# A strip of scratch memory, a reordered key product and weight loads one step ahead, in a fused attention and channel-mix kernel

## The chip, the core and the metric

The kernel runs on one core of a Trainium2 chip. The metric is device time in microseconds (us): the median over runs of the whole program. Five engines work side by side: PE multiplies matrices, DVE, ACT and POOL work elementwise, SP issues most of the DMA transfers. Each runs its own instructions in the order in which they stand in the program, and waits for others by semaphores.

## The reference

```python
def _attn_ref(q, k, v, cap):                     # 8 batches, 12 heads, 448 positions, 64 wide
    scores = (1 / sqrt(64)) * q @ k.T
    scores = cap * tanh(scores / cap)
    attn = softmax(scores)                       # 1e-9 added to the sum
    return attn @ v
def _moe_ref(x, mu_k, mu_r, w_k, w_v, w_r):      # x: 8 x 448 x 768, the attention's output
    xk = mu_k * x + (1 - mu_k) * x_prev          # x_prev: the position before
    xr = mu_r * x + (1 - mu_r) * x_prev
    v = relu(xk @ w_k) ** 2 @ w_v                # 768 -> 1024 -> 768
    return sigmoid(xr @ w_r) * v
```

The weights come as 64-bit floats, and the kernel turns them into 32-bit ones itself.

## The kernel before

**Pairs and steps.** Two heads make a pair: six pairs to a batch, 48 in all. The main loop in `run` has 55 steps. A step `i` works on several pairs at once, and a string (`STEP_0` for steps 0 to 5, `STEP_6` for 6 to 14, `STEP` after that) lists by hand the order in which its operations are written on the engines:

- `S0` to `S3` (`scores`) are the scores of pair `i` on PE, `tanh` and `exp` the two passes over them on ACT, `red` the row sums on DVE, `V` (`values`) the product with v of pair `i - 1`;
- `gather`, `recip`, `rec_store` and `rec_load` carry the row sums of pair `i - 1` through DMA to DVE and back;
- `norm`, `mix_old`, `mix_new`, `x_high`, `x_low` make `xk` of pair `i - 2` and split it, on POOL, into a high part `xkh` and a low part `xkl`; `gate_old` (POOL) and `gate_new` (DVE) make `xg`, and `x_store` writes that, or for 14 pairs the raw `x`, to memory (tensor `raw_d`).

**The key product.** `K` stands four times in a step. Each call of `kpart` (L367) does 6 of a batch's 144 passes: for each of 8 column blocks `fc` and each of 6 pairs `dc` of the batch three matmuls, (wh, xh), (wl, xh) and (wh, xl). `key_order` lists the passes. A batch's first six passes are done by the last `K` of step 6b+6, passes 6 to 29 by the four of step 6b+7, passes 30 to 35 by the first of step 6b+8. The sixth pair of batch b is mixed and split in step 6b+7. When a column block is done, `relu` takes it out of its PSUM buffer on ACT (tile `ko`, L374); there are two such buffers (`kps`), so block 2 can begin when block 0 is out.

**Weights.** `w_k` comes in 11 pieces, at steps 0 to 10; `w_r` and `w_v` in 28, at steps 15 to 42. In its step a piece is loaded by SP near the step's start (`weight_load`, tile `w64`, three buffers; L398 or L403), and ACT takes its absolute value at the step's end (`weight_abs`, L410, into `wsq`), just ahead of the next step's first `tanh`. DVE's five operations on it (`f`, L429 to L437) and POOL's sum (L444) follow in the next step.

**The end of attention.** Behind the last pair the pools of attention are closed, and `w2_prep` makes 7 combinations of blocks of `w_v` in high and low parts (`wvh`, `wvl`), on ACT (L490) and DVE (L491), with two scratch tiles `w2s` of 3072 bytes a partition. They lie where the pools `up` and `xp` lay: `up` takes 5632 bytes, and behind it in `xp` lie `x0` and `x1`, which `x_store` still reads for pairs 46 and 47. A scratch tile waits for what used its bytes before. The last batch's key passes run meanwhile; then 112 units of products with `w_v` and `w_r` (`multiply`, L559) fill PE to the end.

Of the kernel before, what the change touches and what calls it, by code (L numbers as in the profile page):

```python
# [10 lines left out]
F32 = mybir.dt.float32  # L11
# [11 lines left out]
ND = DM // 128  # L23
# [6 lines left out]
P = 128  # L30
# [7 lines left out]
KEYS, REST = range(NWK), range(15, 15 + (ND + NF) * 2)  # L38
# [33 lines left out]
class Body:  # L72
# [263 lines left out]
    def key_order(self, last):  # L336

        t = lambda fc, d0, d1: [(fc, dc, p) for dc in range(d0, d1) for p in range(3)]
        e = ND - 1
        if last:  # L340
            new = t(0, 0, e - 1) + t(1, 0, e - 1) + t(0, e - 1, e) + t(1, e - 1, e) + t(2, 0, e) + t(3, 0, 3) \
                + t(0, e, ND) + t(1, e, ND) + t(3, 3, e) + t(2, e, ND) + t(3, e, ND)
            rest = range(4, NF)
        else:
            new = t(0, 0, e) + t(1, 0, e) + t(0, e, ND) + t(1, e, ND)
            rest = range(2, NF)
        return new + [x for fc in rest for x in t(fc, 0, ND)]

# [56 lines left out]
        self.w_next = n + 1  # L405

    def weight_abs(self):
        for n, w in self.w_raw:
            sq = self.wp.tile([P, WC], F32, name="wsq", bufs=3)[:, :w.shape[1]]
            self.nc.scalar.activation(sq, w[:, :, 1].bitcast(F32), AF.Abs)  # L410
            self.w_abs.append((n, w, sq))
        self.w_raw, self.w_goal = [], self.w_next

    def weight_rest(self):
        while self.w_used < self.w_goal:
# [236 lines left out]
    def step(self, i, KS):  # L652

        nk = 0
        if self.maxima and i < NPAIR:
            self.row_maxima(i)
        pair = dict(load_qk=i + 3, qk_high=i + 2, qk_low=i + 2, qk_rise=i + 2, load_v=i, S=i, tanh=i, exp=i, red=i)
        pair.update(dict.fromkeys("V gather recip rec_store rec_load".split(), i - 1))
        pair.update(dict.fromkeys("norm mix_old mix_new x_high x_low gate_old gate_new x_store".split(), i - 2))
        for op in (STEP_0 if i < 6 else STEP_6 if i < REST[0] else STEP).split():  # L660
            j = pair.get(op)
            op, g = (op[:-1], (int(op[-1]),)) if op[-1].isdigit() else (op, ())
            if op in pair:
                j = pair[op] if j is None else j
                if 0 <= j < NPAIR:
                    getattr(self, dict(S="scores", V="values").get(op, op))(j, *g)
            elif op == "K":
                n = ((i - LAG) * 4 + nk + 1) * KS
                if 0 <= n < B * NF * ND * 3:
                    self.kpart(n, n + KS)  # L670
                nk += 1
            elif op == "tail_open":
                self.tail_open(i)
            elif op == "f":
                if i <= NPAIR:
                    self.fill()
            elif op == "weight_load":
                if i in KEYS or i in REST:
                    self.weight_load()
            else:  # L680
                getattr(self, op)()

    def run(self):
# [7 lines left out]
        with ExitStack() as outer:  # L691
            def pool(name, bufs, stack=outer, **kw):
                return stack.enter_context(tc.tile_pool(name=name, bufs=bufs, **kw))
# [16 lines left out]
            xkp1 = pool("xkp1", 1, kst)  # L710
            self.up = pool("up", 2, ust)
            xp = pool("xp", 1, ust)
            self.xkp = [pool("xkp0", 1, est), xkp1]
            self.wp = pool("wp", 1, wst)
            self.rawp = pool("rawp", 2, ast, **right)
# [13 lines left out]
            self.qk_high(1)  # L729
            self.qk_low(1)  # L730
            self.load_qk(2)
            self.wgen = self.weight_round()
            self.W2, self.b12, self.src, self.ss, self.ops, self.ps, self.ev, self.got, self.vl = ({} for _ in range(9))
            tail = NPAIR + 1
# [123 lines left out]
```

## Time and profile before

| what | value |
|---|---|
| median of 3 runs | 931.31 us (930.99 to 934.17) |
| profiled execution, its own time | 934.75 us |
| its span, first to last instruction | 932.9 us |
| PE busy | 895.6 us, 96% |
| DVE busy | 734.8 us, 79% |
| ACT busy | 640.9 us, 69% |
| POOL busy | 384.2 us, 41% |

The span is what the rows of a trace add up to; 1.85 us of the profiled execution lie outside it. The profiled execution took 3.4 us more than the median. Starts and durations below are in us from the span's start. Busy PE is not PE at its peak, since the ends of matmuls are modelled and overlap.

### The profile page before, as it was taken

How to read it: one execution, taken by the hardware profiler on the slowest of the kernel's cores; microseconds unless marked ns; L12 is line 12 of the kernel's file. 1: busy time of each engine (PE TensorE's matmuls, PEld its weight loads, DVE VectorE, ACT ScalarE, POOL GpSimd, SP SyncE). 2: the span in 40 equal slices, each digit the busy share in tenths (PEclk: the TensorE clock that was granted, in tenths of full speed). 3: DMA queues.
4: the chain of work that ended last, by engine and by line, in shares of the span. 5: the costliest groups of instructions: out<-in, count | busy, mean ns of one | idle time of the engine just before them, and what ended most of it. 6: DMA issues, size and time to landing. Idle time of an engine off the chain costs nothing.

```text
span 932.9 us, 15106 instructions
## 1 busy us (share of the span) xinstructions
PE 895.6 (96%) x4986; PEld 718.0 (77%) x4986; DVE 734.8 (79%) x1254; ACT 640.9 (69%) x947; POOL 384.2 (41%) x329
## 2 busy tenths in 40 slices
PE   6888999999999999999999989999999999999996
PEld 3335766666676666666666778999999999999996
DVE  7999886878888888888877468788887766877775
ACT  6898888787787788878787456565655535555553
POOL 4564463666676676666664200000000013344430
PEclk9899999999999999999999989999999999999999
DMA  4556554566655666656653372754445636666663
GB/s 143 167 173 189 188 174 150 186 186 205 203 196 192 204 212 204 211 179 201 196 180 119 114 277 96 254 182 145 158 157 162 195 110 202 216 212 220 221 216 111
DMA packets 122567, 170.37 MB, mean 183 GB/s; under 512 B 22512, under 2 KB 106608, under 8 KB 122480
## 3 DMA queue, kind: packets, MB, share of 16 engines
q1 hardware_dynamic: 113264, 154.64, 52.5%
q10 hardware_dynamic: 9216, 14.68, 4.2%
q8 instruction: 41, 0.67, 0.3%
q14 instruction: 46, 0.38, 0.1%
HBM read 109.91 MB, written 56.60 MB: 178 GB/s over the span
## 4 chain that ended last, share of the span: by engine, by line
PE 42%; POOL 19%; DVE 11%; DMA 9%; issue 9%; SPq 5%; ACT 3%; ACTq 0%; DVEq 0%; POOLq 0%
PE ps L559 37%; POOL xg L311 5%; POOL qkl L96 5%; DMA sq<-r 4%; POOL xkl L96 4%; SPq L258 4%; PE kps L367 2%; DVE r L253 2%; POOL qkh L86 2%; POOL xkh L86 2%; POOL wsq L444 2%; DMA w<-wk 2%; DVE sr L262 2%; PE s L209 1%; DVE xg L305 1%
## 5 line engine op out<-in xcount | busy, mean ns | idle before, releaser
L253 DVE TRANSPOSE_TENSOR_REDUCE r<-p 128x28 f32<-128x896 f32 (+1 forms) x240 | 215.3, 911 | 11.6 <-ACT p L227 8.6
L227 ACT ACTIVATE p<-p,cap_t 128x896 f32<-128x896 f32 x192 | 182.2, 949 | 6.6 <-ACT pv L288 1.5
L217 ACT ACTIVATE p<-s,scl_t 128x896 f32<-128x896 f32 x192 | 173.1, 901 | 18.3 <-PE s L209 14.1
L367 PE MATMUL kps<-xkh,wkh 128*128 128x448 f32 x372 | 142.9, 384 | 8.8 <-ACT ko L374 8.2
L367 PE MATMUL kps<-xkh,wkl 128*128 128x448 f32 x372 | 137.4, 369 | 0.1
L367 PE MATMUL kps<-xkl,wkh 128*128 128x448 f32 x372 | 137.3, 369 | 0.0
L559 PE MATMUL ps<-wvh,hi 128*128 128x384 f32 x392 | 131.2, 335 | 1.8 <-ACT hi L543 1.2
L559 PE MATMUL ps<-wvl,hi 128*128 128x384 f32 x392 | 131.0, 334 | 0.0
L236 PE MATMUL pv<-p,rv 128*64 128x448 f32 x576 | 125.3, 572 | 1.4 <-DVE xk L293 1.4
L543 ACT CAST hi<-s 128x512 fp32r<-128x512 f32 (+1 forms) x112 | 63.6, 568 | 90.9 <-PE ps L559 76.6
L523 POOL TENSOR_TENSOR s<-src 128x384 f32<-128x384 f32 x14 | 14.3, 1021 | 268.7 <-DVE lo L544 257.2
L544 DVE TENSOR_TENSOR lo<-s,hi 128x512 fp32r<-128x512 f32 (+1 forms) x112 | 70.5, 629 | 57.6 <-ACT hi L543 41.8
L96 POOL TENSOR_TENSOR qkl<-rqk,qkh 128x960 fp32r<-128x960 f32 x47 | 106.3, 2261 | 17.0 <-ACT qkh L90 8.8
L209 PE MATMUL s<-qkh 64*128 64x448 f32 (+1 forms) x336 | 84.3, 441 | 17.5 <-ACT p L217 11.3
L444 POOL TENSOR_TENSOR wsq<-wa,wsq 128x384 f32<-128x384 f32 (+1 forms) x39 | 43.8, 1124 | 135.2 <-DVE wsq L437 135.2
L559 PE MATMUL ps<-wrh,hi 128*128 128x384 f32 x294 | 98.6, 335 | 0.3 <-DVE o L582 0.3
L559 PE MATMUL ps<-wrl,hi 128*128 128x384 f32 x294 | 98.5, 335 | 0.0
L209 PEld LDWEIGHTS s<-qkh 64*128 64x128 f32 (+1 forms) x336 | 37.0, 188 | 75.1 <-ACT p L217 28.9
L367 PEld LDWEIGHTS kps<-xkh,wkh 128*128 128x128 f32 x372 | 70.8, 190 | 30.1 <-issue 13.1
L543 ACT CAST hi<-src 128x512 fp32r<-128x512 f32 (+1 forms) x84 | 47.6, 567 | 62.3 <-PE ps L559 59.6
L236 PEld LDWEIGHTS pv<-p,rv 128*64 128x64 f32 x576 | 38.9, 142 | 65.2 <-issue 59.8
L559 PE MATMUL ps<-wvh,lo 128*128 128x384 f32 x392 | 83.7, 334 | 0.0
(96 smaller groups left out, 1786.7 us busy)
## 6 DMA issues: line engine op xcount, KB each, us to landing
rqk<-qk SPq DMA_DIRECT2D x47, 480.0 KB
k_d<-ko ACTq DMA_DIRECT2D x64, 224.0 KB
src<-k_d SPq DMA_DIRECT2D x56, 256.0 KB
rv<-v SPq DMA_DIRECT2D x48, 256.0 KB
r<-rec_d SPq DMA_DIRECT2D x96, 112.0 KB
v_d<-o SPq DMA_DIRECT2D x56, 192.0 KB
src<-x_d SPq DMA_DIRECT2D x42, 256.0 KB
vl<-v_d SPq DMA_DIRECT2D x56, 192.0 KB
```

Source lines behind the costliest of these rows:

```text
L96: {"p": self.nc.gpsimd, "v": self.nc.vector}[e].tensor_sub(*a)
L209: nc.tensor.matmul(s[:, h, 0:S], qk[a][p, k], qk[b][p, 0:S], start=(n == 0), stop=(n == 2))
L217: self.nc.scalar.activation(p32, self.S.pop((i, g))[:, :n, 0:S], AF.Tanh, scale=self.scl_t)
L227: self.nc.scalar.activation(p32, p32, AF.Exp, scale=1.0 if self.maxima else self.cap_t)
L236: nc.tensor.matmul(pv[p, 0:S], v[:, g, h, :], ph[:, h, :], start=(g == 0), stop=False)
L253: self.nc.vector.tensor_reduce(out=out, in_=p32[p, h].rearrange("p h (b k) -> p (h b) k", k=32), axis=mybir.AxisListType.X, op=ALU.add, ap ...
L311: self.nc.gpsimd.tensor_scalar(self.xg, self.X[i % 2][:, 0:S], self.om["r"][:, i % NP:i % NP + 1], None, op0=ALU.mult)
L367: nc.tensor.matmul(self.kps[fc][:, 0:S], w, m[:, dc, :], start=first, stop=last)
L444: {"p": self.nc.gpsimd, "v": self.nc.vector}[e].tensor_add(sq, f(a), sq)
L543: self.nc.scalar.copy(hi, x)
L544: self.nc.vector.tensor_sub(lo, x, f(hi))
L559: self.nc.tensor.matmul(o, a[:, c, :], w[:, c, :], start=first and k == 0, stop=last and k == len(todo) - 1, skip_group_check=True)
```

## The change

```diff
         else:
-            new = t(0, 0, e) + t(1, 0, e) + t(0, e, ND) + t(1, e, ND)
+            new = t(0, 0, e) + t(1, 0, e - 1) + t(0, e, ND) + t(1, e - 1, ND)
             rest = range(2, NF)
...
     def weight_abs(self):
-        for n, w in self.w_raw:
+        for n, w in [self.w_raw.pop(0)]:
...
             self.w_abs.append((n, w, sq))
-        self.w_raw, self.w_goal = [], self.w_next
+            self.w_goal = n + 1
...
             elif op == "weight_load":
+                if i + 1 in KEYS or i + 1 in REST:
+                    self.weight_load()
+            elif op == "weight_abs":
                 if i in KEYS or i in REST:
-                    self.weight_load()
+                    self.weight_abs()
...
             xp = pool("xp", 1, ust)
+            xp.tile([P, P], F32, name="apart")
...
             self.load_qk(2)
+            self.weight_load()
```

Three things change. A tile `apart` of 512 bytes a partition, which nothing uses, goes in front of `x0`. In batches 0 to 6 the second column block's passes for the fifth pair move behind the first block's passes for the sixth pair, so that pass 27 is the first that reads the sixth pair, where it was pass 30. And each weight piece is loaded one step earlier than its `weight_abs`, the first ahead of the loop.

On PE, in step 7 (6b+7 for batch 0), the last nine of the 24 passes before the two scores of step 8. The tile `kps` is a column block's buffer; before, all are of block 1 (`kps_896`):

```order
L367 MATMUL kps_896<-xkh_420,wkh_123 128x448
L367 MATMUL kps_896<-xkh_420,wkl_124 128x448
L367 MATMUL kps_896<-xkl_421,wkh_123 128x448
L367 MATMUL kps_896<-xkh_420,wkh_123 128x448
L367 MATMUL kps_896<-xkh_420,wkl_124 128x448
L367 MATMUL kps_896<-xkl_421,wkh_123 128x448
L209 MATMUL s_939<-qkh_773 128x448 x2
```

and now the last three are of block 0 (`kps_799`):

```order
L367 MATMUL kps_899<-xkh_423,wkh_123 128x448
L367 MATMUL kps_899<-xkl_424,wkh_123 128x448
L367 MATMUL kps_799<-xkh_423,wkh_123 128x448
L367 MATMUL kps_799<-xkh_423,wkl_124 128x448
L367 MATMUL kps_799<-xkl_424,wkh_123 128x448
L209 MATMUL s_945<-qkh_776 128x448 x2
```

Those last three are passes 27 to 29, block 0 with the sixth pair: they finish block 0 here, and stand in front of all that PE does in the next step.

On ACT, from the end of step 7 to the third tanh of step 8 (`p` are the probabilities, `wsq` the absolute value of a weight piece, `ko` a column block taken out of PSUM), before:

```order
L227 ACTIVATE p32_1_917<-p32_1_917,cap_t_172 128x448
L410 ACTIVATE wsq_922<-w64_822 128x768
L217 ACTIVATE p32_2_978<-s_939,scl_t_174 128x896
L227 ACTIVATE p32_2_978<-p32_2_978,cap_t_172 128x896
L217 ACTIVATE p32_2_984<-s_946,scl_t_174 128x896
L227 ACTIVATE p32_2_984<-p32_2_984,cap_t_172 128x896
L90 CAST qkh_987<-rqk_924 128x960
L217 ACTIVATE p32_2_995<-s_964,scl_t_174 128x896
L374 ACTIVATE ko_997<-kps_796 128x448
L374 ACTIVATE ko_999<-kps_896 128x448
```

and now:

```order
L227 ACTIVATE p32_1_920<-p32_1_920,cap_t_173 128x448
L374 ACTIVATE ko_925<-kps_799 128x448
L380 DMA k_d_63<-ko_925 128x448
L410 ACTIVATE wsq_928<-w64_725 128x768
L217 ACTIVATE p32_2_984<-s_945,scl_t_175 128x896
L227 ACTIVATE p32_2_984<-p32_2_984,cap_t_173 128x896
L217 ACTIVATE p32_2_990<-s_952,scl_t_175 128x896
L227 ACTIVATE p32_2_990<-p32_2_990,cap_t_173 128x896
L90 CAST qkh_993<-rqk_930 128x960
L217 ACTIVATE p32_2_1001<-s_970,scl_t_175 128x896
L374 ACTIVATE ko_1003<-kps_899 128x448
```

Block 0's `ko` has moved from behind the third tanh of step 8 to the end of step 7, in front of the weight piece's absolute value and of the first tanh of step 8.

On SP, in front of and within step 0 (`rqk` is q and k of a pair, `rv` its v, `w64` a weight piece, `sq` the gathered row sums), before:

```order
L159 DMA rqk_213<-qk 128x960
L163 DMA rv_215<-v 128x512
L398 DMA w64_217<-wk 128x3x256
L159 DMA rqk_267<-qk 128x960
L258 DMA sq_0_197<-r1_0_193 32x112 x4
```

and now:

```order
L159 DMA rqk_214<-qk 128x960
L398 DMA w64_216<-wk 128x3x256
L163 DMA rv_218<-v 128x512
L398 DMA w64_220<-wk 128x3x256
L159 DMA rqk_270<-qk 128x960
L258 DMA sq_0_198<-r1_0_194 32x112 x4
```

One piece more is loaded at the start, and from then on the load at the same place in a step is that of the next piece.

## Rows read from the trace of the kernel before

**Rows 1.** The page: shares of the span on the ending chain, by engine and line.

```profile
PE ps L559 37%; POOL xg L311 5%; POOL qkl L96 5%; DMA sq<-r 4%; POOL xkl L96 4%; SPq L258 4%; PE kps L367 2%; DVE r L253 2%; POOL qkh L86 2%; POOL xkh L86 2%; POOL wsq L444 2%; DMA w<-wk 2%; DVE sr L262 2%; PE s L209 1%; DVE xg L305 1%
```

**Rows 2.** Waits of PE: us in total, times, longest.

```profile
PE kps L367 <- ACT ko L374: 8.2, 3, 4.4
```

**Rows 3.** Timeline of PE, end of attention: start, us, [idle before <-releaser].

```profile
543.82 0.37 PE L367 MATMUL s<-xkl,wkh 128*128 128x448 f32 x1
548.62 0.74 PE L367 MATMUL kps<-xkh,wkh 128*128 128x448 f32 x1 [4.44 <-ACT ko L374]
...
565.89 0.37 PE L367 MATMUL kps<-xkl,wkh 128*128 128x448 f32 x1
567.47 0.45 PE L559 MATMUL ps<-wvh,hi 128*128 128x384 f32 x1 [1.21 <-ACT hi L543]
```

**Rows 4.** Timelines of SP, DVE and ACT, end of attention.

```profile
533.22 4.16 SPq L479 DMA_DIRECT2D wvl<-w_d  x8
537.43 1.05 SPq L324 DMA_DIRECT2D raw_d<-x  x2
...
545.57 0.96 DVE L491 TENSOR_TENSOR w2s<-wvl,w2s 128x768 f32<-128x768 f32 x1 [4.05 <-DMA raw_d<-x]
...
548.03 0.97 ACT L374 ACTIVATE ko<-kps 128x448 f32<-128x448 f32 x2
...
555.35 0.55 ACT L374 ACTIVATE ko<-kps 128x448 f32<-128x448 f32 x1 [0.97 <-PE kps L367]
...
557.16 0.96 DVE L491 TENSOR_TENSOR wvl<-wvl,wvh 128x768 fp32r<-128x768 f32 x1 [2.39 <-ACT wvh L490]
```

**Rows 5.** Stretches: us, busy PE, PEld, DVE, ACT, POOL (instructions), PEclk, DMA, GB/s.

```profile
536.00:543.00 7.00, 7.00 (x36) 6.36 (x35) 2.72 (x4) 2.31 (x3) 1.71 (x2) 1.00 1.03 364
549.00:554.00 5.00, 5.00 (x14) 4.43 (x14) 4.88 (x7) 4.04 (x8) 0.00 (x0) 0.50 0.84 287
```

**Rows 6.** Timelines: pass 29 on PE, sixth pair's `xkl` on POOL, steps 7, 13, 43.

```profile
80.61 0.36 PE L367 MATMUL kps<-xkl,wkh 128*128 128x448 f32 x1
...
84.56 1.16 POOL L96 TENSOR_TENSOR xkl<-xk,xkh 128x448 fp32r<-128x448 f32 x1
...
151.21 0.37 PE L367 MATMUL kps<-xkl,wkh 128*128 128x448 f32 x1
...
151.83 1.16 POOL L96 TENSOR_TENSOR xkl<-xk,xkh 128x448 fp32r<-128x448 f32 x1
...
478.35 0.36 PE L367 MATMUL kps<-xkl,wkh 128*128 128x448 f32 x1
...
480.24 1.15 POOL L96 TENSOR_TENSOR xkl<-xk,xkh 128x448 fp32r<-128x448 f32 x1
```

**Rows 7.** Waits of DVE, whole run, and the last of them on its timeline.

```profile
DVE xg L305 <- POOL xg L311: 26.9, 29, 1.1
...
524.51 0.68 DVE L305 SCALAR_TENSOR_TENSOR xg<-x,mu_r,xg 128x448 f32<-128x448 f32 x1 [0.95 <-POOL xg L311]
```

**Rows 8.** Waits of ACT, whole run, for the pieces of the key weights.

```profile
ACT wsq L410 <- DMA w<-wk: 5.9, 3, 2.4
```

**Rows 9.** Stretch from step 4 to step 11, columns as in group 5.

```profile
41.00:128.00 87.00, 76.35 (x410) 46.65 (x407) 79.91 (x128) 72.67 (x89) 48.35 (x41) 0.94 0.61 191
```

**Rows 10.** Timelines of PE and ACT, steps 3 and 4.

```profile
42.83 1.01 PE L236 MATMUL pv<-p,rv 128*64 128x448 f32 x2 [1.37 <-DVE xk L293]
...
48.68 1.01 ACT L217 ACTIVATE p<-s,scl_t 128x896 f32<-128x896 f32 x1 [0.58 <-PE s L209]
```

**Rows 11.** Timeline of ACT, ends of steps 7 and 10, and the chain's load.

```profile
83.90 0.95 ACT L410 ACTIVATE wsq<-w 128x768 f32<-128x768 f32 x1 [1.79 <-DMA w<-wk]
84.75 0.98 ACT L217 ACTIVATE p<-s,scl_t 128x896 f32<-128x896 f32 x1
...
120.99 0.96 ACT L410 ACTIVATE wsq<-w 128x768 f32<-128x768 f32 x1 [1.71 <-POOL qkl L96]
...
115.99 4.91 DMA w<-wk
```

## What the change will do to the time

> **What bounds the kernel now.** I read first the shares of the chain that ended last [rows 1]. Outside the products at the end (PE, L559, 37%) it runs through POOL's `xg`, `qkl`, `xkl`, `xkh` and `qkh`, the DMA of the row sums and SP's issue of it, and DVE's `r` and `sr`; PE's K passes and scores hold 2% and 1%. PE is nearly always busy, but in attention it is held to the pace of POOL, DVE and the row sums' DMA; at the end it is the bound itself. The list of waits has PE waiting for `ko` 8.2 us in three places, the longest 4.4 [rows 2]. The reader is to see where each sits and who is late there. A K pass that comes late in attention costs only what the other engines don't have in hand; a stop at the end costs in full.
>
> All sums are against the profiled execution's 934.75 us and are then laid on the median, 931.31, 3.4 lower.
>
> **The strip.** DVE's operation on the second scratch tile starts at 545.57, after 4.05 us idle for the DMA `raw_d<-x` [rows 4]. That store is issued by SP at 537.43, behind eight loads of `wvl` from 533.22 on, in the same queue. `w2s` takes 6144 bytes, `up` 5632: the second scratch lies 512 bytes deep in `x0`. With the strip of 512 bytes in front it ends where `x0` begins, and the wait for the store goes; left is that for the third of the eight loads. What follows from the 4.05 us now: ACT's high part waits for `w2s`, its two `ko` start at 548.03 behind it, PE has stopped after 544.19 and goes on at 548.62 with 4.44 us idle [rows 3, 4]. I take the DVE wait, **−4.1**, and what lies behind it: at 555.35 ACT waits 0.97 us for PE [rows 4], which a PE that comes earlier takes away, **−1.0**; together **−5.1**. Lower bound of the gain 4.1. Upper: PE's whole 4.44 and the clock behind it. In 549 to 554 the granted clock is 0.50, 1.2 GHz; 14 passes take 5.00 us, 0.36 each, where 536 to 543 at 1.00 shows 36 in 7.00, 0.19 each [rows 5]. Some 15 passes at 0.165 more are 2.5 us; so 4.44 + 2.5 = 7.0. I stay near the lower end because DVE and ACT share the work with the passes there (2.39 us of DVE waiting for ACT's `wvh` at 557.16 stay [rows 4]).
>
> The Trainium skill has a rule on this (Perfetto Trace Analysis, Matmul Optimizations): the matmul engine scales its power with use, so matmuls should run back to back. The 0.50 after the 4.44 us stop agrees with it. By that rule alone the term would be −7.0, by the row of DVE's wait −5.1.
>
> **27 passes.** Now PE's last three passes of step 6b+7 wait for the sixth pair's high and low part, with the next step's scores, values and K passes queued behind them. Against the trace: pass 29 starts at 80.61 in step 7, `xkl` of the sixth pair ends at 84.56 + 1.16 = 85.72, 5.1 us later. In step 13 it is 151.21 against 152.99, 1.78; in step 43, 478.35 against 481.39, 3.04 [rows 6]. The four batches between give 2.45, 2.11, 1.32 and 1.72 by the same rows. PE would stand still for these, 12.4 us in the six after the first.
>
> How much of it reaches the end? The steps from 15 to 47 run in a ring without PE: POOL's `xg`, DVE's `xg`, row sums out and back through DMA, DVE's reciprocal and `xk`, POOL's `xkh`, `xkl`. The chain says so [rows 1], and so does DVE's `xg`: it waits for POOL's 29 times, 26.9 us in all, 0.9 a step, and still 0.95 in one of the last [rows 7]. That is what DVE has in hand; PE, which feeds the row sums DVE works on, may fall behind by as much without the ring noticing. A stall only sets PE to the ring's time, and the next one is then measured from there; so they don't add up. The last counts: 3.04 less 0.95, **+2.1**. Bounds: 0, if the ring goes on untouched, and +12.4, if each is kept.
>
> Step 7 is not in that ring: there the start-up's pace still holds. ACT too is now queued there: `ko` of block 0 waits for pass 29, and behind it stand the piece's absolute value and the first tanh of step 8. 85.72 + 0.37 (pass) + 0.55 (`ko`, as at 555.35 [rows 4]) + 0.95 (`wsq` [rows 11]) and 0.4 for issuing its store, an estimate, is 88.0 against 84.75 for that tanh [rows 11]: **+3.2**, in round numbers 3. Doing `ko` here also spares ACT and PE their later waits for block 0 (PE's for `ko` in rows 2 are the two besides 4.44, 8.2 − 4.4 = 3.8); they lie inside the stall, and I count nothing for them.
>
> **Weights a step ahead.** The same pieces at the same place in SP's queue, one earlier in name; one more load, ahead of the loop. The buffers (three `w64`) suffice, as a piece is read one step after its load. SP's other transfers keep their order, except that one piece goes ahead of `rv` at the start and none is left for steps 10 and 42. That piece is 128 × 768 words, 393 KB, and at the 364 GB/s of [rows 5] takes 1.1 us; values are wanted a step later than scores, so I put it at nothing, with a bound of +1.1. What goes is ACT's waits for `w<-wk`: 5.9 us in three [rows 8], 2.4, 1.8 and 1.8, and 1.71 more in step 10, which the row puts down to POOL but where the chain shows the load, 115.99 + 4.91 = 120.90, against 120.99 [rows 11]. Which are worth something? The first lies in step 3: V of that step starts at 42.83 after DVE's `xk`, and a tanh of step 4 waits for PE at 48.68 [rows 10]; hidden. Those at steps 6 and 7 lie in front of the stall above, which ends later than they did; hidden. The last counts, −1.7. Thus the early part is 3.0 − 1.7 = **+1.3**. Bounds: between 41 and 128 DVE is busy 79.91 of 87.00 [rows 9], so at most −7.1 by freeing ACT; above, the stall at its full 5.1 with nothing back.
>
> The Trainium skill says to issue a DMA early and wait late, so that its fixed cost lies behind compute (DMA: Bandwidth & Descriptors, Rules for kernel authors). If all four waits came off the end, that would be 5.9 + 1.7 = 7.6; DVE's 7.1 caps it.
>
> **Sum:** −5.1 + 1.3 + 2.1 = **−1.7**: 933.05 for this execution, and 931.3 − 1.7 = **929.6** for the median.
>
> **Rivals.**
> *B, the stalls vanish.* With the loads early, POOL's and DVE's chain up to `xkl` also moves forward in steps 3 to 10, the stall at step 7 shrinks with it, and the middle stalls stay within what the ring has in hand. Then −7.1 and −5.1 remain: 931.3 − 12.2 = 919; with the stall half there, 922. For it: four waits on one engine's way [rows 8, 11]. Against: DVE's share [rows 9], tanh already waiting for PE in step 4 [rows 10].
> *C, slower: each stall is kept.* PE's standstill delays scores and with them DVE's row sums, by more than the 0.95 us that DVE's `xg` has in hand [rows 7]; then POOL, released by the same `xg`, is as late in each batch. +12.4 + 1.3 − 5.1 = +8.6: 939.9. It decides from a stall of 0.95 on; all six are over it [rows 6]. Against: a step's row sums are gathered only in the next step, so a late score has time. A fallen clock behind each stall, as in 549 to 554 [rows 5], would add to it.
> *D, the strip does nothing.* DVE waits in place of the store for the third `wvl` load, issued at about 534.5; if its landing is as late as the store's, the 5.1 stay: 931.3 + 1.3 + 2.1 = 934.7. Against: the eight loads are issued over 4.16 us, and the store comes behind all of them [rows 4]: five loads stand between the third and the store.
>
> **How the numbers follow.** A, the forecast, 0.52: 929.6, its own range 926 to 933.5 (the strip at 7.0 and the last stall at 0 make −1.9 − 2.1 more, 925.6; the middle at +6 makes 933.5). B 0.28, 919 to 922. C 0.12, around 939.9. D 0.08, 934.7. A difference of 0.5% (4.7 us) is about what a measurement can tell from none; the borders are 926.65 and 935.97. Faster: B, and 0.06 of A with both good ends, 0.34. Slower: C and a little of D, 0.13. Same: the rest, 0.53. The range from 920 to 937 leaves out the better third of B and most of C, 0.2.
>
> **What would show it.** Right: no wait of DVE L491 for `raw_d`, PE's stop before block 2 in the last batch gone or under 1 us, granted clock 1.00 there; PE's K passes wait for POOL `xkl` seven times, the first about 5 us, the sum of the rest less than 12; DVE's `xg` wait for POOL falls in number; ACT's waits for `w<-wk` gone. Wrong: the first slots' start (567.47 before [rows 3]) moves by more than 5 us, either way; a new wait of DVE for a load at the end; POOL waiting for DVE in the step after each stall (C); step 11's start 5 us or more earlier (B).

## The result and the profile after

The changed kernel takes **940.08 us** (median of 7 runs, 935.70 to 943.18), the kernel before 932.79 in the same count of runs: a ratio of **1.0076** (95% interval 1.0050 to 1.0102), 7.1 us slower. The forecast was 929.6 us, with a range of 920 to 937, counted from a median of three runs of the kernel before, 931.31 us; that of seven is 1.5 us higher. The profiled execution took 943.18 us, its span is 941.3 us; it is 3.1 us above its median, and we shall see where these come from. One of the ten runs of e10 (below), 1697.4 us, was in a slow state and is left out of its ratio.

The waits of PE, whole run (us in total, times, longest). There were none for `xkh` and `xkl` before, and the 8.2 us for `ko` [rows 2] have become 2.6:

```profile
PE kps L367 <- POOL xkh L86: 8.8, 4, 5.2
PE kps L367 <- POOL xkl L96: 3.0, 6, 0.6
PE kps L367 <- ACT ko L374: 2.6, 2, 1.5
```

The first two rows are the new stops in front of pass 27 and of pass 29, 11.8 us together. The timelines of PE and ACT show them (start, us, [idle before <-releaser]), in step 7, two of those behind it, and at the end:

```profile
87.70 0.74 PE L367 MATMUL kps<-xkh,wkh 128*128 128x448 f32 x1 [5.17 <-POOL xkh L86]
...
223.07 0.47 PE L367 MATMUL kps<-xkh,wkh 128*128 128x448 f32 x1 [1.52 <-POOL xkh L86]
...
224.32 0.47 PE L367 MATMUL kps<-xkl,wkh 128*128 128x448 f32 x1 [0.56 <-POOL xkl L96]
...
487.32 0.47 PE L367 MATMUL kps<-xkh,wkh 128*128 128x448 f32 x1 [1.83 <-POOL xkh L86]
...
488.56 0.55 PE L367 MATMUL kps<-xkl,wkh 128*128 128x448 f32 x1 [0.56 <-POOL xkl L96]
...
575.54 0.44 PE L559 MATMUL ps<-wvh,hi 128*128 128x384 f32 x1 [2.17 <-ACT hi L543]
...
89.71 0.54 ACT L374 ACTIVATE ko<-kps 128x448 f32<-128x448 f32 x1 [5.13 <-PE kps L367]
...
90.75 0.91 ACT L410 ACTIVATE wsq<-w 128x768 f32<-128x768 f32 x1 [0.50 <-ACT ko L374]
91.56 0.99 ACT L217 ACTIVATE p<-s,scl_t 128x896 f32<-128x896 f32 x1
```

And the stretches around the first stop, columns as in group 5 of the rows of before: the granted clock (the figure behind the five engines) is 0.50, 1.2 GHz, behind it. Between 93 and 545 us it falls only once more, to 0.50 from 489 to 492, behind the last of these stops.

```profile
80.00:87.00 7.00, 2.52 (x13) 2.00 (x11) 6.86 (x11) 4.46 (x6) 4.72 (x3) 0.93 0.65 205
87.00:92.00 5.00, 4.19 (x15) 2.60 (x15) 2.97 (x5) 1.80 (x3) 1.79 (x3) 0.50 0.70 214
```

The lists of DVE's and POOL's waits tell who else is late. `r`, the row sum of a pair's probabilities, waits for ACT more than twice as often as before, and POOL's `xkh` waits for `xk` 30 times for 21; the forecast named POOL's wait as a sign of rival C. `xg` hands back only 3.4 of its 26.9 us [rows 7] and waits as often as before. The rows of the changed kernel:

```profile
DVE xg L305 <- POOL xg L311: 23.5, 29, 1.1
DVE r L253 <- ACT p L227: 19.5, 31, 1.4
POOL xkh L86 <- DVE xk L293: 55.1, 30, 7.0
```

And of the kernel before:

```profile
DVE r L253 <- ACT p L227: 8.6, 13, 1.1
POOL xkh L86 <- DVE xk L293: 48.2, 21, 6.8
```

At the end DVE's 4.05 us for `raw_d` and PE's 4.44 us stop [rows 3, 4] are gone, and new waits stand there, on ACT's and DVE's timelines:

```profile
554.27 0.97 ACT L374 ACTIVATE ko<-kps 128x448 f32<-128x448 f32 x2
557.05 1.08 ACTq L380 DMA_DIRECT2D k_d<-ko  x2
558.18 1.57 ACT L490 CAST wvh<-w2s 128x768 fp32r<-128x768 f32 x2 [2.94 <-DMA src<-k_d]
...
559.77 1.83 DVE L491 TENSOR_TENSOR wvl<-w2s,wvh 128x768 fp32r<-128x768 f32 x2 [2.42 <-ACT wvh L490]
```

To see where the time went, the same events are laid side by side: the end of `xkl` on POOL, pair by pair, the first product of the end on PE, and the span. Pairs are counted from 1 in this table, so that pairs 12, 42 and 48 are a batch's sixth. The last kernel is the changed one with the old order of passes (e4, below).

| event | before | after | e4 | after − before | after − e4 |
|---|---|---|---|---|---|
| `xkl` of pair 5 | 72.30 | 75.48 | 73.24 | +3.2 | +2.2 |
| pair 8 | 109.50 | 116.68 | 109.36 | +7.2 | +7.3 |
| pair 12 | 152.98 | 156.86 | 151.57 | +3.9 | +5.3 |
| pair 42 | 481.39 | 488.50 | 479.25 | +7.1 | +9.3 |
| pair 44 | 503.25 | 513.13 | 501.13 | +9.9 | +12.0 |
| pair 48 | 539.47 | 549.84 | 537.56 | +10.4 | +12.3 |
| first product of the end | 567.47 | 575.54 | 564.06 | +8.1 | +11.5 |
| span | 932.9 | 941.3 | 929.2 | +8.4 | +12.1 |

So, by the last column, the time goes in step 7, slowly through the middle and in the last batch but one; the end gives 2.3 us back (567.47 − 539.47 = 28.0 before, 25.7 now). The 3.2 us at pair 5, ahead of every moved pass, are an execution's own: the changed kernel and e5 (below) have the same instructions up to step 12, and there pair 5's `xkl` ends 2.8 us earlier, at 72.67. Their rows for 60 to 68 us, first of the changed kernel, then of e5, differ in the granted clock:

```profile
60.00:68.00 8.00, 5.74 (x22) 1.92 (x26) 7.77 (x15) 6.05 (x9) 4.74 (x4) 0.63 0.68 206
```

```profile
60.00:68.00 8.00, 7.33 (x37) 3.38 (x38) 6.76 (x14) 7.07 (x9) 4.90 (x5) 0.79 0.70 216
```

That is about the profiled execution's distance to its median, 3.1 us, and it is left out of what follows.

### The profile page after: what moved, and what is told of

Read it like the earlier page. It is cut to its first block, busy times and chain, and to the rows that moved or that the text cites. A ratio compares the mean times of both kernels' runs of the same rounds, so it can differ in the third digit from the quotient of the medians.

```text
span 941.3 us, 15079 instructions
## 1 busy us (share of the span) xinstructions
PE 897.6 (95%) x4986; PEld 717.1 (76%) x4986; DVE 738.5 (78%) x1254; ACT 643.0 (68%) x947; POOL 384.0 (41%) x329
## 4 chain that ended last, share of the span: by engine, by line
PE 49%; DVE 14%; POOL 13%; DMA 7%; issue 6%; SPq 5%; ACT 4%; DVEq 0%; ACTq 0%; POOLq 0%
PE ps L559 37%; DMA sq<-r 4%; SPq L258 4%; PE kps L367 4%; PE pv L236 4%; POOL xg L311 4%; POOL xkl L96 4%; PE s L209 4%; DVE r L253 3%; POOL qkl L96 2%; DVE sr L262 2%; POOL xkh L86 2%; DVE xk L293 2%; DVE xg L305 2%; ACT p L217 1%
## 5 line engine op out<-in xcount | busy, mean ns | idle before, releaser
L217 ACT ACTIVATE p<-s,scl_t 128x896 f32<-128x896 f32 x192 | 173.0, 901 | 23.6 <-PE s L209 20.6
L367 PE MATMUL kps<-xkh,wkh 128*128 128x448 f32 x372 | 141.2, 380 | 11.5 <-POOL xkh L86 8.8
```

The costliest lines, as they stand in the source:

```text
L217: self.nc.scalar.activation(p32, self.S.pop((i, g))[:, :n, 0:S], AF.Tanh, scale=self.scl_t)
L367: nc.tensor.matmul(self.kps[fc][:, 0:S], w, m[:, dc, :], start=first, stop=last)
```

## The experiments

Three theories of the loss stood against one another. P: the moved passes alone make it. W: the weights a step ahead make a part of it. And within P: L, the forecast's, that only the last stall counts, against K, that each stall is kept. Each comparison is with the kernel before, run in turn on the same chip (934.2 to 934.9 us there), e1 to e8 on one chip and e9 to e12 on another. Four kernels take the change apart.

**e1_strip**: the tile `apart` alone.

```diff
             xp = pool("xp", 1, ust)
+            xp.tile([P, P], F32, name="apart")
```

> The strip alone, the rest as before. Theory P (the passes' order makes the loss) and theory W (the weights a step ahead make a good part of it) agree here: in the changed kernel the way from the last xkl to the first product of the end took 25.7 us for 28.0 before, so -2 us against before, 930.5 or so, and no DVE wait for raw_d. The forecast had -5.1. If the strip only gains behind the other changes, 0.

Measured: 0.9987 (0.9966 to 1.0007), −1.2 us, which can't be told from none.

**e2_p27**: the passes alone.

```diff
-            new = t(0, 0, e) + t(1, 0, e) + t(0, e, ND) + t(1, e, ND)
+            new = t(0, 0, e) + t(1, 0, e - 1) + t(0, e, ND) + t(1, e - 1, ND)
```

> The 27 passes alone. Theory P: all of the loss ahead of the end is this edit's, +5 by step 8, +2 in the middle, +3 in the last batch, so +10 us at the last xkl and, with the old 4 us wait at the end, about +9 to +10, 942. Theory W: the stall at step 7 is shorter or absorbed, since the delay of 3.2 us that stood before the first moved pass (xkl of the fifth pair) is the weights': +5 to +7, 938 to 940.

Measured: 1.0078 (1.0055 to 1.0100), +7.3 us, between what P and what W expected.

**e3_weights**: the weights a step ahead alone (the rest of the change's diff).

> The weights a step ahead alone. Theory P: 0 or a gain of 1 to 2 us (four waits of ACT gone). Theory W: PE's values of steps 3 and 5 run at the granted clock's half again and xkl of the fifth pair is about 3 us late, so +2 to +4 us, 935 to 937.

Measured: 0.9969 (0.9951 to 0.9987), −2.9 us. W falls: the loads ahead gain.

**e4_strip_weights**: strip and weights, the passes as before.

> The changed kernel with the old order of passes. Theory P: -2 us, 930.5, the stalls for xkh and xkl gone and with them all of the loss. Theory W: +1 us, 934: the early 3 us stay, the strip gives 2 back. Between this and the changed kernel lies what the passes cost: 9 to 10 us by P, 6 by W.

Measured: 0.9957 (0.9940 to 0.9973), −4.0 us. On top of these two edits the passes cost 1.0076 − 0.9957, 1.2% or 11.1 us, and alone 7.3. P holds.

Next, which of the seven stalls are kept. Strip and weights stay, and the new order of passes is used in some batches only.

```diff
-    def key_order(self, last):
+    def key_order(self, last, early):
...
-        else:
+        elif early:
             new = t(0, 0, e) + t(1, 0, e - 1) + t(0, e, ND) + t(1, e - 1, ND)
             rest = range(2, NF)
+        else:
+            new = t(0, 0, e) + t(1, 0, e) + t(0, e, ND) + t(1, e, ND)
+            rest = range(2, NF)
...
-        self.order = [self.key_order(b == B - 1) for b in range(B)]
+        self.order = [self.key_order(b == B - 1, b == 0) for b in range(B)]
```

(`0 < b < 6` in e6, `b == 6` in e7, for `b == 0` in e5.)

**e5_first_batch**

> Strip and weights as changed, 27 passes in batch 0 alone, 30 in the others. Theory L (the forecast's: a stall sets PE to the others' pace, so that only what is late in the last batch counts): the stall in step 7 is made up on the way, -4 us against before, as with no moved pass at all (e4_strip_weights). Theory K (PE and the ring of POOL, DVE and the row sums wait for one another, and each stall is kept): +3 us on that, -1 us against before, since xkl of the eleventh pair came 3 us later against e4_strip_weights beyond what was there at the sixth.

**e6_middle**

> The same with 27 passes in batches 1 to 5 alone. Theory L: 0 on the -4, so -4 us: none of these stalls is the last. Theory K: five stalls, together 4 us in the changed kernel's list of PE's gaps, +4 on the -4, so 0 against before.

**e7_sixth**

> The same with 27 passes in batch 6 alone. Both theories: +2 to +3 on the -4, so -1 to -2 us against before, with a stall of 2 to 3 us at step 43. By K the three sum to the changed kernel's 11 us over e4_strip_weights; by L this one alone makes what there is, and the rest of the 11 stays without a cause.

| kernel | batches with 27 | ratio to before | interval | us over e4 |
|---|---|---|---|---|
| e4 | none | 0.9957 | 0.9940 to 0.9973 | 0 |
| e5 | 0 | 1.0000 | 0.9982 to 1.0017 | +4.0 |
| e6 | 1 to 5 | 1.0000 | 0.9982 to 1.0019 | +4.0 |
| e7 | 6 | 0.9971 | 0.9955 to 0.9987 | +1.3 |
| after | 0 to 6 | 1.0076 | 1.0050 to 1.0102 | +11.1 |

Each ratio is against its own runs of before, and the last column has some 2.3 us to either side (2.9 for the changed kernel). e6 decides for K against L: its five stalls, none of them in the last place, cost 4 us where L has nothing. e5 agrees with K (3 expected), and e7's 1.3, where both theories had 2 to 3, can't be told from none. The three sum to 9.3 of the 11.1; the rest is within the intervals.

Why is a stall kept? Either because PE has nothing in hand to make it up with (K1), or because it makes others late (K2). Two kernels with less work for PE tell these apart.

```diff
-            nc.tensor.matmul(self.kps[fc][:, 0:S], w, m[:, dc, :], start=first, stop=last)
+            if t != 1 or dc not in (1, 4) or b == B - 1:
+                nc.tensor.matmul(self.kps[fc][:, 0:S], w, m[:, dc, :], start=first, stop=last)
```

**e9_less_pe**: on e4.

> e4_strip_weights with less work for PE: in batches 0 to 6 the product (low weights, high x) of two of the six pairs is left out, 16 of a batch's 144 passes, 0.204 us each, 22.8 us of PE in all; the key product is less exact by it. Theory F (the forecast's: the ring of POOL, DVE and the row sums sets the pace in the middle and PE has only to keep up): -4 us against before as without, at most -6. Theory P (PE sets the pace, or has as little in hand as the ring): well beyond, -10 to -25 us.

Measured: 0.9919 (0.9895 to 0.9942), −7.6 us, 3.6 less than e4 for 22.8 us less of PE. So PE does not set the pace there. It is a little beyond what F expected, and well short of this expectation's P.

**e10_middle_less_pe**: on e6.

> The same passes left out, and 27 passes in batches 1 to 5 as in e6_middle. Both orders now give PE 3.3 us in hand in each batch. Theory K1 (a stall is kept because PE has nothing in hand to make it up with): no difference from e9_less_pe, within 1.5 us. Theory K2 (the moved passes make scores late and lengthen the ring itself): 4 us or more slower than e9_less_pe, as e6_middle was than e4_strip_weights, since PE comes to pass 27 earlier and waits longer there.

Measured: 1.0040 (1.0013 to 1.0067), +3.7 us, **11.3 us slower than e9_less_pe**. K1 expected no difference. With 3.3 us in hand in each batch PE comes earlier and waits longer, and more is lost than before, not less; but the clock has a part in that, as its rows below show. The timelines of e10 around its longest stop, PE, ACT, DVE and POOL in this order (the program has four lines more above these passes):

```profile
283.48 0.74 PE L371 MATMUL kps<-xkh,wkh 128*128 128x448 f32 x1 [3.88 <-POOL xkh L86]
...
287.91 2.95 PE L236 MATMUL pv<-p,rv 128*64 128x448 f32 x12
...
285.48 0.54 ACT L378 ACTIVATE ko<-kps 128x448 f32<-128x448 f32 x1 [3.40 <-PE kps L371]
...
286.94 1.00 ACT L217 ACTIVATE p<-s,scl_t 128x896 f32<-128x896 f32 x1
...
292.61 1.01 ACT L217 ACTIVATE p<-s,scl_t 128x896 f32<-128x896 f32 x1 [1.63 <-PE s L209]
...
294.27 0.63 ACT L288 ACTIVATE pv<-x,om_k 128x448 f32<-128x448 f32 x1
...
291.01 1.11 DVE L253 TRANSPOSE_TENSOR_REDUCE r<-p 128x28 f32<-128x896 f32 x1 [0.57 <-ACT p L227]
...
294.93 0.68 DVE L293 SCALAR_TENSOR_TENSOR xk<-x,mu_k,pv 128x448 f32<-128x448 f32 x1 [1.21 <-ACT pv L288]
...
295.70 0.57 POOL L86 TENSOR_SCALAR xkh<-xk 128x448 fp32r<-128x448 f32 x1 [1.91 <-DVE xk L293]
```

Read from above, each engine in its own order: PE stops for `xkh`; scores and values of the next step stand behind the passes; the third tanh waits 1.63 us for scores; `mix_old` (`pv`, L288) stands behind that tanh on ACT; DVE's `xk` waits for it 1.21 us, and `r` for ACT 0.57; POOL's `xkh` waits 1.91 for `xk`. The stop has come round to the engine that caused it. The granted clock around it:

```profile
270.00:279.00 9.00, 9.00 (x52) 6.16 (x51) 7.79 (x13) 7.18 (x10) 5.60 (x7) 1.00 0.55 192
283.00:290.00 7.00, 6.41 (x25) 3.48 (x27) 5.55 (x10) 4.00 (x6) 3.45 (x4) 0.58 0.64 206
```

The granted clock is 1.00 ahead of the stop and 0.58 in the seven us around its end; the 12 matmuls of V take 2.95 us here, 3.43 to 4.03 behind the other four stops, and 2.48 in the steps at 1.00. The Trainium skill says that the matmul engine scales its power with use (Perfetto Trace Analysis, Matmul Optimizations); this row agrees.

How much of the 11.3 us is the clock? Between 93 and 545 us it is at 0.50 for 31 us in e10, some of it behind each of the five stops, and for 3 us in e9. A pass takes 0.36 us at 0.50 and 0.19 at 1.00 [rows 5]; by that, an estimate, PE does some 13 us less work in the difference, as much as the whole loss. So e10 alone does not decide between K1 and K2.

The length of a step does. This is the time in us from the end of the sixth pair's `xkl` to the end of the next pair's, across the stops of batches 1 to 5; the clock is 1.00 in all of them but those of e10 and, for 3.4 us, step 37 of e9:

| step | before | e4 | e9 | e6 | after | e10 |
|---|---|---|---|---|---|---|
| 13 | 10.84 | 10.78 | 10.96 | 12.20 | 12.20 | 13.58 |
| 19 | 11.94 | 11.82 | 10.54 | 11.29 | 11.28 | 13.57 |
| 25 | 10.53 | 10.55 | 10.54 | 11.28 | 11.28 | 12.87 |
| 31 | 10.55 | 10.56 | 10.54 | 11.27 | 11.26 | 13.93 |
| 37 | 10.56 | 10.56 | 10.54 | 11.28 | 11.27 | 13.79 |

With the old order it is the same from step 25 on with all of PE's work (e4) and with 3.3 us less of it in each batch (e9), so that PE's lack of reserve is not what holds it. With the new order it is 0.7 us longer, behind a stop of 0.3 us as behind one of 1.5, at the full clock. So it is not a stall's length that is kept: each stop makes the next round of the ring longer, and K2 holds. The five steps are 3.1 us longer in e6 than in e4, most of its 4.0. In e10 they are longer again by 1.4 to 2.7 us, with the clock at 0.50 in each.

The way round at the full clock is a shorter one than in e10. PE, DVE and POOL in step 25 of the changed kernel and behind it:

```profile
290.24 0.47 PE L367 MATMUL kps<-xkl,wkh 128*128 128x448 f32 x1 [0.55 <-POOL xkl L96]
...
296.28 1.11 DVE L253 TRANSPOSE_TENSOR_REDUCE r<-p 128x28 f32<-128x896 f32 x1 [0.59 <-ACT p L227]
...
299.65 0.57 POOL L86 TENSOR_SCALAR xkh<-xk 128x448 fp32r<-128x448 f32 x1 [0.56 <-DVE xk L293]
```

And DVE and POOL at the same place in e4, without either wait:

```profile
287.81 2.10 DVE L253 TRANSPOSE_TENSOR_REDUCE r<-p 128x28 f32<-128x896 f32 x2
...
292.28 0.57 POOL L86 TENSOR_SCALAR xkh<-xk 128x448 fp32r<-128x448 f32 x1
```

Pass 29 waits for `xkl`. Behind it stand the next step's scores on PE and `ko` on ACT, and behind these ACT's `tanh` and `exp`; DVE's second `r` waits for that `exp`, and behind `r` on DVE stand `x`, `sr` and `xk`.

**e12_ko_late**: the changed kernel, with block 0's `ko` on ACT back behind the third tanh of the next step.

```diff
-        for b, fc, ps in self.done:
+        now = [x for x in self.done if x[1] or x[0] == B - 1 or x in self.held]
+        self.held = self.done = [x for x in self.done if x not in now]
+        for b, fc, ps in now:
```

> The changed kernel, all its passes as moved, but block 0's ko stays on ACT where it was, behind the third tanh of the next step. If the loss is PE's standstill: as the changed kernel, +6 to +8 us against before. If ACT's queue behind the early ko (its store, the piece's absolute value, the next tanh) makes it: at most +2.

Measured: 1.0091 (1.0058 to 1.0124), +8.5 us. ACT's early `ko` and what is queued behind it cost nothing of their own that could be seen; PE's standstill does. ACT now waits at the next tanh instead: 48.2 us for scores, 46 times, where the changed kernel has 20.6 us for scores and 33.5 in front of its `ko`. And steps 25 and 31 take 11.22 and 11.20 us here, nearly as with the early `ko`: the late scores are enough.

The other question is where the strip's 5 us are. In e4 the end looks as in the changed kernel; ACT, DVE and PE:

```profile
542.00 0.97 ACT L374 ACTIVATE ko<-kps 128x448 f32<-128x448 f32 x2
545.58 1.08 ACTq L380 DMA_DIRECT2D k_d<-ko  x2
546.70 1.57 ACT L490 CAST wvh<-w2s 128x768 fp32r<-128x768 f32 x2 [3.73 <-DMA src<-k_d]
...
548.30 1.83 DVE L491 TENSOR_TENSOR wvl<-w2s,wvh 128x768 fp32r<-128x768 f32 x2 [3.22 <-ACT wvh L490]
...
564.06 0.44 PE L559 MATMUL ps<-wvh,hi 128*128 128x384 f32 x1 [2.17 <-ACT hi L543]
```

Two `ko` are done at 542.97, and their stores are issued only at 545.58, with the next `wvh` behind them. In the program these stores wait for two of the eight semaphores that the DMAs use in turn, and the last that used them are two of the eight loads `src<-k_d`, which SP issues from 537.26 on. Before, `ko` was 4 us later, counted from the last `xkl`, and its stores left at once:

```profile
548.60 0.81 ACTq L380 DMA_DIRECT2D k_d<-ko  x2
```

e1, which has the strip too, shows the wait as e4 does, 3.70 us. So the issue of the store waits for a landing that has nothing to do with its data. The last batch's stores are therefore given to POOL, which is idle there.

```diff
-            self.nc.scalar.dma_start(self.k_d[fc, :, b * S:(b + 1) * S], ko)
+            queue = self.nc.gpsimd if b == B - 1 else self.nc.scalar
+            queue.dma_start(self.k_d[fc, :, b * S:(b + 1) * S], ko)
```

**e8_store_pool**: on e4.

> Strip and weights as changed, 30 passes, and the last batch's ko written to memory by POOL's queue instead of ACT's. Theory S (the strip's gain is lost because ACT's issue of a k_d store waits for the landing of src loads, in whose rotation of semaphores it stands, with three wvh copies behind it): ACT's 3 us and DVE's 2.4 us of waiting there go, the first product of the end comes 2 to 3 us earlier after the last xkl, -6 to -7 us against before. Rival (DVE's and ACT's work on the w_v combinations fills the stretch anyway): -4, as without.

Measured: **0.9903** (0.9873 to 0.9933), −9.1 us, 5.0 beyond e4: 925.34 us, and the fastest here. ACT goes on behind `ko`, and POOL has the stores:

```profile
539.30 0.97 ACT L374 ACTIVATE ko<-kps 128x448 f32<-128x448 f32 x2
540.16 0.83 ACT L491 CAST wvh<-w2s 128x768 fp32r<-128x768 f32 x1
...
540.14 1.28 POOL L381 DMA_DIRECT2D k_d<-ko  x2 [5.27 <-ACT ko L374]
...
558.07 0.44 PE L560 MATMUL ps<-wvh,hi 128*128 128x384 f32 x1 [1.65 <-ACT hi L544]
```

From the last `xkl` (534.87) to the first product it is 23.2 us, where e4 has 26.5: 3.3 less, a little over theory S's 2 to 3. What else these two executions differ by stands ahead of the edit (the last `xkl` comes 2.7 us earlier than in e4), so that the traces put 3.3 of the 5.0 us down to the store. The Trainium skill says that spreading DMAs over the issuing engines doesn't give bandwidth and only saves the sequencer's time in issuing (DMA: Bandwidth & Descriptors, Rules for kernel authors). No run here tests the bandwidth. What was saved is ACT's time at an issue, as it says, but most of that was a wait and no issuing: of e4's 3.7 us 2.6 lie between the end of `ko` and the first issue.

**e11_no_strip_pool**: e8 without the strip.

> e8_store_pool without the strip. If the strip's term was right and only masked by ACT's wait for the store's turn, DVE's 4 us wait for raw_d is back and counts in full: 4 to 5 us slower than e8_store_pool, -4 to -5 against before. If the strip is worth no more than the 1 to 1.5 us between e1_strip or e4_strip_weights and their counterparts: -8 against before.

Measured: 0.9970 (0.9949 to 0.9991), −2.8 us, 6.3 slower than e8. DVE's wait and PE's stop are back (DVE, PE):

```profile
538.88 0.96 DVE L492 TENSOR_TENSOR w2s<-wvl,w2s 128x768 f32<-128x768 f32 x1 [3.71 <-DMA raw_d<-x]
...
541.93 0.74 PE L367 MATMUL kps<-xkh,wkh 128*128 128x448 f32 x1 [4.47 <-ACT ko L374]
...
559.02 0.45 PE L560 MATMUL ps<-wvh,hi 128*128 128x384 f32 x1 [0.25 <-ACT hi L544]
```

From its last `xkl` (533.11) to the first product this execution, the fastest of its kernel, takes 25.9 us, 2.7 more than e8. The runs say 6.3, with some 3.4 us to either side, and the traces 2.7, at the edge of that. The expectation's first case, a strip that was only masked, had 4 to 5; its second, 1 to 1.5, lies outside the interval. Without the strip the moved store gives nothing by the runs (−2.8, and −2.9 in e3): the two work together. With the store on ACT the strip was worth 1.2 (e1 against before) and 1.1 us (e4 against e3).

## Why the prediction was wrong

**The strip, −5.1 forecast, −1.2 measured**, with an interval of 1.9 us to either side. The wait for `raw_d` and PE's stop went as forecast. The step that failed is "what lies behind it": that the work would simply move forward by DVE's 4.1 us. ACT's two `ko` came forward to the time at which the `src` loads were still landing, and their stores waited for these, 2.9 us on ACT and 2.4 on DVE behind it. That is the wait in the place of the one removed, of which rival D spoke; but it was put at the third `wvl` load on DVE, and sat on ACT. With the store moved the strip gives 2.7 to 6.3 us.

**The weights, −1.7 forecast, −2.9 measured.** ACT's waits for `w<-wk` are gone. One of the four was counted and three were put at nothing; that holds to 1.2 us, with an interval of 1.7 us to either side.

**Step 7, +3.0 forecast, +4.0 measured** (e5 against e4). The stop of 5.17 us was forecast as 5.1; it is 4.49 in e5 and, without strip and weights, 1.27 in e2, so that its size was hit in part by luck. The issue of `ko`'s store, put at 0.4 without a row, takes 0.36 in e5. Together with the weights the early part is +1.1, as against +1.3.

**The middle and the last batch, +2.1 forecast.** This is the step that made the forecast wrong: "a stall only sets PE to the ring's time, and the next one is then measured from there; so they don't add up". The parts measure +4.0 (batches 1 to 5) and +1.3 (batch 6), and the changed kernel leaves 11.1 − 4.0 = 7.1 for them. Half of the step was right: stalls do become smaller behind the first (the six are 6.6 us together, not 12.4, by the gaps on PE's timeline), and the ring, not PE, sets the pace (e9). Wrong was that PE stands outside the ring. Once pass 29 waits for `xkl` with the next step's scores behind it, these hold up ACT's `exp` and DVE's `r`, which stands in front of `x`, `sr` and `xk`, and the next `xkl` comes 0.7 us later than it would, 1.2 to 1.4 in step 13, whatever the length of the stop; these amounts add up. The clock adds to that where it falls, behind each stop of e10 and, in the changed kernel's profiled execution, behind the stops of steps 7 and 43.

**The rivals.** C had the direction of this mechanism, PE's standstill that delays scores and row sums, and the price, +8.6 and 939.9 us, at a chance of 0.12; measured are +7.1 and 940.08. That the price came so near is luck: stalls are half as long and are not kept by their length, the strip gave a quarter, and the median of before lay 1.5 us higher than the one it was counted from. "A step's row sums are gathered only in the next step, so a late score has time" was the sentence that spoke against it; the queue order of DVE gives no such time, since `r` stands there in front of `xk`. B's gains are there only without the passes.

**Open.** The passes cost 7.3 us alone and 11.1 on top of strip and weights; the parts sum to 9.3. In the changed kernel's profiled execution the step from the stop of step 43 on takes 12.69 us, with the clock at 0.50 for 3.4 of them, and 11.23 in e7 at 1.00; that would fit, but it is one execution, and no run separates it from the spread of the runs. Why step 19 takes 11.8 to 11.9 us in before and e4 and 10.54 in e9 (the table behind e10) is open too.

## What to carry to other kernels

A stall that is put on an engine which seems to follow a ring of others must be traced through each queue behind it to the next member of that ring; slack in one wait (`xg`'s 0.9 us) says nothing of the other waits that the same engine will get. So don't put the work whose operand comes last in front of the operations on which others depend. When a loss is to be divided between a wait and a fallen clock, compare the same step in kernels at the same clock. And where a wait is removed, ask what the earlier work will meet: here it was a store's turn among loads. By the traces the stretch from the last `xkl` to the first product is 28.0 us before, 26.4 with the strip, 25.9 with the store moved, and 23.2 with both; by the runs the moved store gains only with the strip.

## What the runs showed of the hardware that was not expected

The same instructions ran with a granted clock of 0.63 in one execution and 0.79 in another between 60 and 68 us, and `xkl` of pair 5 came 2.8 us apart; in start-up, where PE has many short idle times, a single profile can't be trusted to 3 us. In e10 a stop of 3.88 us in the middle of a stretch at 1.00 was followed by a granted clock of 0.58 over the next seven us, and the clock fell to 0.50 behind all five of its stops; behind the five of e6, at the same places, it stayed at 1.00.

ACT stood 3.7 us at the issue of two stores, because their semaphores were still those of loads from another queue that had not landed (e4).
